# Batch 2's queries and keys by fp16 copies and transposed loads, and a new written order for the first part of a fused attention and MLP kernel

## The chip, the cores and the metric

The kernel runs on one core of a Trainium2 chip. The core has a matrix engine (TensorE, PE in the profile), VectorE (DVE), ScalarE (ACT), GpSimd (POOL) and SyncE (SP). DMAs are issued from queues of these engines; here POOL issues all loads that change fp32 into fp16, and SP the transposed loads and the stores. Sixteen DMA engines carry the data of all queues. The metric is the device time of one execution in microseconds.

## The reference

Eight batches, twelve heads, 448 positions and 64 numbers per head; then 3584 tokens of width 768 through an MLP with 2048 hidden units.

```python
scores = scale * np.matmul(q, k.transpose(0, 1, 3, 2))
m = np.max(scores, axis=-1, keepdims=True)
e = np.exp(scores - m)
attn = e / (np.sum(e, axis=-1, keepdims=True) + np.exp(-m) + 1e-09)
out = np.matmul(attn, v)
x = out.transpose(0, 2, 1, 3).reshape(B * S, H * D)
h = np.maximum(x @ w_in, 0.0)
return (h * h) @ w_out
```

The kernel takes the exponentials without the maximum, adds one to their sum (which is the same ratio), and takes the reciprocal as exp(-ln(...)).

## The kernel before, in words

All matmuls are in fp16, and everything is written out by hand: the schedule is manual, so each engine does its instructions in the order in which the program makes them. That order stands in two strings, `ORDER` (line 676) for the first part, called the front here, and `CYCLE` (line 750) for the rest. Each word of a string is a step, a letter with numbers, looked up in `STEPS` (line 637 for the front, line 732 in `period` for the cycle). `ORDER` holds attention of batches 0 to 3, the first layer of batches 0 and 1, and the output pieces 0 to 13. `CYCLE` is run twice, each time for attention of two more batches, the first layer of two earlier ones and 28 output pieces; what is then left is written as plain loops.

The steps that matter here:

- `T` (`transpose_one`, line 203) and `U` (`transposed_copy`, line 210): one quad is a group of four heads, so a batch has three. `T` transposes the queries or the keys of a quad on TensorE, 14 transposes into PSUM; `U` copies them out, on VectorE or ScalarE, into a batch's `qk` tile.
- `s` and `e`: scores of one chunk (64 keys of four heads) and their exponentials. `s0` to `s23` are batch 0's in halves. From 24 on there are seven per quad, so `s24` to `s44` are batch 1, `s45` to `s65` batch 2, `s66` to `s86` batch 3. Chunk c of a quad is its first step plus c. `quad_scores` (line 400) has two forms. A batch in `ON_PE` uses four matmuls of 448 columns a chunk. The others use eight of 224, as their planes hold even and odd positions apart; keys are read from planes 1 and 2, queries from plane 0, and the last chunk's keys from a separate tile `kms`.
- `a`, `S`, `Z`, `M`, `v`, `X`: the sums of exponentials (VectorE and TensorE), their logarithm and reciprocal (ScalarE), the product with the values (TensorE) and the normalised result (VectorE). Their number is that of the quad, with 0 to 2 for batch 1, 3 to 5 for batch 2 and 6 to 8 for batch 3. Batch 0 has its own letters, `p`, `b`, `y`, `z`, `n`, `x`.
- `j`, `k`, `l`: first layer, two of six products of a 128-wide block, then its relu and its square. `j0` to `j15` are batch 1, from `j16` on batch 0. `i`, `r`, `g` do the same for pairs of blocks of half of batch 0.
- `o`, `O`, `Q`: an output piece of 128 tokens and half the width, which takes 16 blocks (two per `o` step in the fine form), and its two-part eviction; `Q` stores from SP. There are four buffers for the evicted pieces.
- `d`: the loads of the list `LOADS` (line 626), by number.

Loads come in two forms. For batches in `ON_PE`, `load_quad` (line 618) brings a quad's queries and keys in natural layout to SBUF by POOL's queue. For the others, `stage` (line 144) copies the whole batch's queries and keys into fp16 tensors in DRAM by POOL's queue, and `transposed_load` (line 163) brings three planes of 0.69 MB (queries, keys, keys shifted by one position) from there by SP's queue. `tail_keys` (line 178) then makes `kms` from planes 1 and 2 by copies on POOL. A batch's `qk` tile has two buffers, so batch b's transposed loads wait for the last scores of batch b-2. The values have two buffers as well, and they take one or three DMAs for a batch in `ON_PE` and four for the others.

A step that issues on POOL or SP stands in that engine's queue of instructions. It is issued as soon as the steps before it on the same engine are done and what it needs is there, wherever it stands among the other engines' steps.

Of the kernel before, what the change touches and what calls it, by code (L numbers as in the profile page):

```python
# [16 lines left out]
def kernel(  # L17
# [160 lines left out]
    def tail_keys(b, planes=(1, 2)):  # L178

        if b not in kms:  # L180
            kms[b] = flat.tile([128, H, 64], FP16, name="flatq")
        km = kms[b]
        for which in planes:
            for r in range(2):
                rows_ = slice(64 * r, 64 * r + 64)
# [2 lines left out]
                nc.gpsimd.tensor_copy(km[rows_].rearrange("p h (x o) -> p h x o", o=2)[:, :, :, odd],  # L188
                                      src[:, :, S // 2 - 32:S // 2])
# [482 lines left out]
    def other_ring():  # L672
# [3 lines left out]
    ORDER = """
        d0 W8 d8 d1 c1,4,0 c0,0,1 t0,0,0 c1,0,1 t1,0,0 u0,0,0,0 t1,0,4 u1,0,0,0 c0,4,1 u1,0,4,1 t0,0,4 d2 s0 t0,1,0 u0,0,4,1 u0,1,0,0 t1,1,0 u1,1,0,0
        d10 d9 s1 t0,1,4 e0 t1,1,4 e1 s2 e2 u0,1,4,0 s12 e12 u1,1,4,0 T0,1,0 T0,1,1 U0,1,0,0,4,0 U0,1,1,0,4,0 U0,1,1,4,7,0 U0,1,0,4,7,0 s3 s4 p2 p0 e3
        b0,0 e4 s6 p1 d18 p3 s5 e6 e5 b0,1 b0,2 T0,2,0 b0,3 y0 T0,2,1 U0,2,0,0,4,0 z0 n0 U0,2,1,0,4,0 b1,0 s8 U0,2,0,4,7,0 U0,2,1,4,7,0 x0 d3 d17 d16
        b1,1 s9 d15 T1,0,1 e8 e9 U1,0,1,0,7,0 T1,0,0 U1,0,0,0,7,0 b2,0 s11 e11 s10 s13 e10 e13 s14 p8 b2,1 p4 d5 b2,2 p9 s7 e14 p10 b2,3 p11 y2 p5 e7  # L680
        z2 b1,2 p6 s15 b1,3 p7 e15 y1 b3,0 n2 x2 b3,1 z1 s17 e17 b3,2 p12 p13 b3,3 n1 s18 p14 s16 e18 p15 x1 y3 T1,1,0 U1,1,0,0,7,0 e16 b4,0 z3 b4,1
        s19 e19 i0,6 n3 r0,6,0 s20 e20 s21 i0,7 s22 x3 b4,2 e21 p16 b4,3 e22 b5,0 r0,7,0 p17 p18 p19 d4 b5,1 g0,6 y4 z4 n4 s23 T1,1,1 e23 d13 s27 b5,2
        x4 i0,4 s28 p20 p21 g0,7 b5,3 e27 p22 p23 y5 U1,1,1,0,7,0 e28 z5 r0,4,0 n5 x5 s26 s29 e26 j20,0,2 j23,0,2 j23,2,4 j20,2,4 j20,4,6 e29 j23,4,6
        s25 k23,1 s24 g0,4 e25 e24 k20,0 P0 i1,7 j19,0,2 l23 a0,0 s32 e32 a0,1 s36 d6 j19,2,4 e36 j16,0,2 l20 j19,4,6 j17,0,2 s34 s33 k19,1 r1,7,0
        j17,2,4 j16,2,4 a0,2 l19 e34 j17,4,6 e33 j16,4,6 g1,7 s30 d11 k16,1 s31 e30 k17,0 T2,0,0 T1,2,0 T2,0,1 T1,2,1 l16 s35 e31 U2,0,0,0,7,0
        U1,2,0,0,7,0 s37 U2,0,1,0,7,1 e35 j18,0,2 j18,2,4 e37 j18,4,6 a0,3 i1,6 d19 S0 U1,2,1,0,7,0 v0,0 a1,0 v0,1 Z0 v0,2 l17 v0,3 v0,4 v0,5 k18,0 d7
        d12 v0,6 s40 s43 M0 r1,6,0 j27,0,2 a1,1 e43 j22,0,2 j22,2,4 j27,2,4 X0 e40 j27,4,6 l18 j22,4,6 g1,6 a1,2 s39 k27,1 s38 e39 a1,3 d20 T2,2,0 e38
        k22,0 T2,2,1 T2,1,1 T2,1,0 s41 U2,2,1,0,7,1 U2,2,0,0,7,0 s42 j26,0,2 l27 e41 j21,0,2 j26,2,4 j26,4,6 l22 S1 U2,1,0,0,7,0 e42 U2,1,1,0,7,0 Z1
        v1,0 v1,1 v1,2 v1,3 v1,4 d23 v1,5 k26,1 v1,6 a2,0 a2,1 a2,2 s44 s47 M1 l26 e44 j21,2,4 d22 j21,4,6 i1,4 X1 a2,3 k21,1 v2,0 v2,1 v2,2 r1,4,0 S2
        e47 v2,3 Z2 v2,4 v2,5 l21 v2,6 M2 o0,0,4 s46 o0,4,8 d14 s50 e46 e50 o0,8,12 X2 o0,12,16 s51 g1,4 s48 O0,1 Q0 j15,0,2 j0,0,2 j15,2,4 j4,0,2  # L690
        j15,4,6 j4,2,4 j4,4,6 j0,2,4 e51 e48 j0,4,6 s45 k15,1 l15 o2,0,4 s49 e45 e49 o2,4,8 s52 d21 o2,8,12 a3,0 e52 o2,12,16 k4,1 k0,0 s53 a3,1 s55
        d24 j10,0,2 O2,1 j1,0,2 Q2 j10,2,4 j1,2,4 j10,4,6 l0 j14,0,2 l4 j1,4,6 j11,0,2 e55 k10,0 j14,2,4 a3,2 j11,2,4 k1,1 j8,0,2 l10 j14,4,6 j11,4,6
        k11,1 j9,0,2 a3,3 j8,2,4 j9,2,4 e53 l1 j8,4,6 j9,4,6 k14,0 s57 l14 e57 l11 S3 Z3 v3,0 d25 v3,1 v3,2 v3,3 k9,0 k8,0 v3,4 v3,5 v3,6 M3 o1,0,4
        s54 o1,4,8 X3 s56 o1,8,12 o1,12,16 e54 a4,0 O1,0 s63 e56 o5,0,4 s58 o5,4,8 Q1 e63 a4,1 a4,2 s65 e58 a4,3 o5,8,12 e65 s60 o5,12,16 e60 O5,1 s59
        v4,0 v4,1 Q5 v4,2 v4,3 l9 S4 v4,4 e59 Z4 M4 v4,5 v4,6 o4,0,4 o4,4,8 s61 o4,8,12 o4,12,16 e61 s64 O4,1 X4 s62 j2,0,2 l8 Q4 j2,2,4 j2,4,6 j7,0,2
        k2,1 j5,0,2 e62 j7,2,4 j7,4,6 k7,0 l7 d27 j12,0,2 j6,0,2 e64 a5,0 j12,2,4 j5,2,4 l2 j5,4,6 k5,1 j6,2,4 j6,4,6 j12,4,6 a5,1 j13,0,2 j13,2,4
        j13,4,6 l5 a5,2 j3,0,2 j3,2,4 j3,4,6 k12,0 a5,3 s69 l12 k6,1 o3,0,4 l6 k13,1 k3,1 l3 S5 l13 o3,4,8 o3,8,12 o3,12,16 O3,0 Q3 e69 s70 Z5 s71 d26
        M5 v5,0 v5,1 v5,2 v5,3 e70 e71 v5,4 v5,5 v5,6 o9,0,2 o9,2,4 X5 o9,4,6 o9,6,8 s66 o9,8,10 s68 o9,10,12 o9,12,14 o9,14,16 e66 O9,0 o6,0,2 e68
        s67 s72 o6,2,4 o6,4,6 o6,6,8 e67 o6,8,10 Q9 a6,0 a6,1 e72 a6,2 s73 o8,0,2 o6,10,12 o6,12,14 o8,2,4 o6,14,16 s75 e73 O6,0 o8,4,6 o8,6,8 e75 s78
        Q6 o8,8,10 o8,10,12 a6,3 e78 o8,12,14 s79 o8,14,16 s77 v6,0 v6,1 v6,2 v6,3 e79 e77 v6,4 S6 v6,5 v6,6 Z6 M6 s74 O8,0 Q8 o7,0,2 o7,2,4 e74 X6  # L700
        o7,4,6 s76 e76 a7,0 o7,6,8 o7,8,10 o7,10,12 o7,12,14 a7,1 o7,14,16 s82 d28 o10,0,2 O7,1 o10,2,4 o10,4,6 Q7 o10,6,8 s80 a7,2 e82 o10,8,10
        o10,10,12 o10,12,14 o10,14,16 e80 s85 s83 o11,0,2 o11,2,4 e85 o11,4,6 o11,6,8 d31 O10,1 Q10 e83 s81 a7,3 d29 o11,8,10 o11,10,12 o11,12,14 e81
        o11,14,16 O11,1 Q11 s84 o12,0,2 s86 o12,2,4 o12,4,6 e84 e86 o12,6,8 o12,8,10 a8,0 o12,10,12 o12,12,14 o12,14,16 S7 a8,1 O12,0 o13,0,4 o13,4,8
        d30 o13,8,12 Z7 Q12 a8,2 o13,12,16 v7,0 v7,1 v7,2 v7,3 O13,1 v7,4 a8,3 v7,5 v7,6 M7 S8 Q13 v8,0 v8,1 Z8 v8,2 v8,3 M8 v8,4 v8,5 X7 v8,6 X8
    """
# [120 lines left out]
```

## Time and profile before

| what | value |
|---|---|
| median of 3 runs | 392.39 us (392.0 to 394.6) |
| the profiled execution, its time | 393.06 us |
| its span in the profile | 391.3 us |
| granted TensorE clock | 1.0 throughout |
| HBM read, written | 45.69 MB, 17.93 MB |

Engine names are those of the profile; PEld is the loading of weights into TensorE. q0 is the DMA queue of POOL, q1 that of SP. The DMA share is the mean busy share of the sixteen DMA engines. It can exceed 1 as packets overlap. The sizes of loads are counted as they arrive, in fp16. In a timeline, a line is a run of like instructions with its start, its length, and in brackets the idle time before it and what ended that. A matmul's duration there reaches past the start of the next one, so the cost of one is taken from start to start.

### The profile page before, as it was taken

The numbers are of one execution on the slowest core, as the hardware profiler recorded it, in microseconds if no ns is written. First come the engines' busy times: TensorE is split into PE (matmuls) and PEld (weight loads), VectorE is DVE, ScalarE is ACT, GpSimd is POOL, SyncE is SP. The second block draws the span as 40 slices with busy tenths as digits, with TensorE's granted clock in tenths as the row PEclk, the third lists the DMA queues.
The fourth block names the chain that finished last, engine by engine and source line by source line (L and its number), as shares of the span: only waits on it lengthen the run. The fifth ranks groups of instructions, "written<-read, shape, count | busy, mean of one in ns | idle before, by whom it ended". The sixth has DMA issues, their size and how long they took to land.

```text
span 391.3 us, 14259 instructions
## 1 busy us (share of the span) xinstructions
PE 383.2 (98%) x6432; PEld 253.7 (65%) x6432; DVE 251.9 (64%) x468; ACT 228.5 (58%) x308; POOL 62.2 (16%) x96
## 2 busy tenths in 40 slices
PE   9789999999999999999999999999999999999997
PEld 5566656565789755667777665667777755556665
DVE  2887995765666766556968757566778788880000
ACT  5999998586689511349988731248988730001221
POOL 8544420025000701300001240310000000000000
PEclk9999999999999999999999999999999999999999
DMA  8999999999939899903129596941112200001132
GB/s 143 203 205 205 202 203 205 182 182 175 215 75 175 158 195 149 160 2 66 44 54 194 145 182 131 151 46 44 52 55 64 64 23 2 0 0 61 62 82 80
DMA packets 75052, 45.34 MB, mean 116 GB/s; under 512 B 47472, under 2 KB 72944, under 8 KB 74992
## 3 DMA queue, kind: packets, MB, share of 16 engines
q0 software_dynamic: 24752, 22.62, 37.4%
q1 hardware_dynamic: 49952, 21.59, 28.1%
q8 instruction: 50, 0.82, 0.9%
q10 hardware_dynamic: 288, 0.23, 0.2%
q14 instruction: 10, 0.08, 0.1%
HBM read 45.69 MB, written 17.93 MB: 163 GB/s over the span
## 4 chain that ended last, share of the span: by engine, by line
PE 86%; ACT 6%; DMA 2%; SPq 2%; DVE 1%; issue 1%; POOL 1%; ACTq 0%; POOLq 0%; DVEq 0%
PE mp L93 77%; PE sp L93 8%; ACT et L254 4%; SPq L166 2%; DMA nn<-in_k_dram 2%; PE mp L207 1%; DMA out_dram<-ot 1%; ACT rcp L372 1%; ACT nn L254 0%; DVE qk L217 0%; ACT rcp L365 0%; ACT ot L575 0%; DVE half L341 0%; ACT rcp L463 0%; DVE half L447 0%
## 5 line engine op out<-in xcount | busy, mean ns | idle before, releaser
L93 PE MATMUL mp<-wout,gs 64*64 64x384 f16 (+2 forms) x2928 | 165.2, 322 | 0.0
L93 PE MATMUL mp<-xt,win 128*64 128x448 f16 (+2 forms) x1188 | 148.3, 347 | 0.1
L93 PEld LDWEIGHTS <-gs 64*64 64x64 f16 (+1 forms) x2928 | 103.1, 106 | 34.5
L93 PEld LDWEIGHTS <-win 128*64 128x64 f16 (+1 forms) x1188 | 83.2, 106 | 63.5 <-issue 4.2
L254 ACT ACTIVATE et<-sp 128x896 f16<-128x896 f32 (+2 forms) x131 | 110.6, 889 | 12.3 <-PE sp L93 11.7
L505 DVE TENSOR_SCALAR rt<-mp 128x448 f16<-128x448 f32 x87 | 54.1, 622 | 17.4 <-PE mp L93 14.5
L509 DVE TENSOR_TENSOR gs<-rt 128x448 f16<-128x448 f16 x128 | 47.8, 390 | 22.1 <-ACT rt L503 20.2
L503 ACT ACTIVATE rt<-mp 128x448 f16<-128x448 f32 x41 | 21.8, 543 | 65.0 <-PE mp L93 55.7
L575 ACT ACTIVATE ot<-mp 128x384 f32<-128x384 f32 (+2 forms) x31 | 14.9, 480 | 71.6 <-PE mp L93 68.8
L93 PE MATMUL sp<-qk 64*64 64x224 f16 (+1 forms) x1056 | 53.7, 274 | 2.1 <-DVE qk L217 0.5
L93 PEld LDWEIGHTS <-qk 64*64 64x64 f16 x1056 | 32.7, 115 | 15.2 <-issue 6.5
L188 POOL COPY flatq<-qk 64x384 f16<-64x384 f16 x20 | 14.8, 739 | 172.7 <-DMA qk<-stage_k 126.0
L254 ACT ACTIVATE nn<-sp 128x896 f16<-128x896 f32 x42 | 37.1, 916 | 4.3 <-PE sp L93 4.2
L487 DVE TENSOR_TENSOR xt<-mp,rcp 128x448 f16<-128x448 f32 x42 | 24.2, 619 | 15.7 <-ACT rcp L466 10.3
L581 DVE SCALAR_TENSOR_TENSOR ot<-mp,ot 128x384 f32<-128x384 f32 x42 | 23.4, 556 | 15.3 <-ACT ot L575 12.4
L93 PEld LDWEIGHTS <-vn 64*64 64x64 f16 x756 | 22.4, 107 | 10.4 <-issue 1.8
L93 PE MATMUL mp<-et,vn 64*64 64x448 f16 (+1 forms) x448 | 24.5, 343 | 0.0
L577 DVE TENSOR_SCALAR ot<-mp 128x384 f32<-128x384 f32 x26 | 14.4, 555 | 14.3 <-PE mp L93 14.2
L463 ACT ACTIVATE rcp<-sp,one_b 128x896 f32<-128x896 f32 x21 | 21.1, 1007 | 2.8 <-PE sp L93 2.7
L466 ACT ACTIVATE rcp<-rcp 128x896 f32<-128x896 f32 x21 | 19.9, 949 | 0.5
L441 DVE TENSOR_TENSOR half<-et 128x1792 f16<-128x1792 f16 x15 | 16.3, 1088 | 4.3 <-ACT et L254 4.2
L443 DVE TENSOR_TENSOR half<-half,et 128x1792 f16<-128x1792 f16 x15 | 16.3, 1086 | 0.3
(59 smaller groups left out, 197.4 us busy)
## 6 DMA issues: line engine op xcount, KB each, us to landing
out_dram<-ot SPq DMA_DIRECT2D x52, 96.0 KB, 2.9
out_dram<-ot SPq DMA_DIRECT2D x19, 192.0 KB, 1.9
win<-in_moe_w_in_dram POOLq DMA_DIRECT2D x8, 384.0 KB, 12.3
wout<-in_moe_w_out_dram POOLq DMA_DIRECT2D x4, 768.0 KB, 14.9
vn<-in_v_dram POOLq DMA_DIRECT2D x10, 288.0 KB, 8.4
stage_q<-in_q_dram POOLq DMA_DIRECT2D x4, 676.0 KB, 13.1
stage_k<-in_k_dram POOLq DMA_DIRECT2D x4, 676.0 KB, 15.9
nn<-in_q_dram POOLq DMA_DIRECT2D x8, 224.0 KB, 8.6
```

The lines of the kernel that those rows point to most:

```text
L93: return nc.tensor.matmul(out_, lhsT, rhs, start=start, stop=stop)
L254: nc.scalar.activation(out=out_, in_=in_, func=AF.Exp, scale=scale)
L441: nc.vector.tensor_add(esq[m], a[:, 0:w], a[:, w:2 * w])
L443: nc.vector.tensor_add(esq[m], esq[m], z[:, 0:w])
L463: nc.scalar.activation(out=rcp, in_=zp[:, :, 0:S], func=AF.Ln, bias=one_b)
L466: nc.scalar.activation(out=zqs[m], in_=zqs[m], func=AF.Exp, scale=-1.0)
L487: nc.vector.tensor_mul(xts[b][:, 2 * g + i, :], xqs[m][i][:, 0:S], zqs[m][:, i, :])
L503: nc.scalar.activation(out=rt[:, 0:m], in_=hp[:, 0:m], func=AF.Relu)
L505: nc.vector.tensor_scalar(out=rt[:, 0:m], in0=hp[:, 0:m], scalar1=0.0, scalar2=None, op0=ALU.max)
L509: nc.vector.tensor_mul(gs[:, f0:f0 + per, t0 % RING:t0 % RING + n], r, r)
L575: nc.scalar.activation(out=ot, in_=op[:, 0:w], func=AF.Copy, scale=OUT_SCALE)
L581: nc.vector.scalar_tensor_tensor(out=ot, in0=lo[:, 0:w], scalar=OUT_SCALE, in1=ot, op0=ALU.mult, op1=ALU.add)
```

## The change

`ON_PE` loses batch 2: `load_quad`, `T` and `U` of batch 2 go, and `stage`, three transposed loads and the tail copies take their place. Batch 2's scores, values and stores take the second form. `LOADS` is made anew, with the transposed loads and the tail copies as steps of their own. `ORDER` is written anew.

```diff
-    ON_PE = (0, 1, 2)
+    ON_PE = (0, 1)
...
         x = {(0, 1): (0, 0), (0, 2): (0, 1), (1, 0): (1, 0), (1, 1): (0, 0), (1, 2): (0, 1),
-             (2, 0): (1, 0), (2, 1): (1, 1), (2, 2): (0, 0)}[b, g]
...
-    LOADS = ([lambda b=b, g=g: load_quad(b, g) for b in range(3) for g in range(NQ) if b + g]
+    LOADS = ([lambda b=b, g=g: load_quad(b, g) for b in range(2) for g in range(NQ) if b + g]
              + [lambda b=b, g=g: load_v_quads(b, g, g + 1) for b in range(2) for g in range(NQ)]
-             + [lambda: load_v_quads(2)]
              + [lambda i=i: load_win(i, NW) for i in range(NW)]
-             + [lambda n0=n0, y=y: load_wout(n0, y, 2) for n0 in (0, HALF) for y in range(2)]
-             + [lambda: stage(3), lambda: transposed_loads(3), lambda: tail_keys(3), lambda: load_v_quads(3),
-                lambda: stage(4), lambda: transposed_loads(4), lambda: tail_keys(4), lambda: load_v_quads(4), lambda: stage(5)])
+             + [lambda n0=n0, y=y: load_wout(n0, y, 2) for n0 in (0, HALF) for y in range(2)])
+    for b in (2, 3, 4):
+        LOADS += [lambda b=b: stage(b), lambda b=b: load_v_quads(b)]
+        LOADS += [lambda b=b, i=i: transposed_load(b, i) for i in range(3)]
+        LOADS += [lambda b=b, i=i: tail_keys(b, (i,)) for i in (1, 2)]
+    LOADS += [lambda: stage(5)]
```

The load numbers mean:

| load | before | after |
|---|---|---|
| quads of batches 0 and 1 (queries and keys) | d0 to d4 | d0 to d4 |
| quads of batch 2 | d5 to d7 | none |
| values of batches 0 and 1 by quads | d8 to d13 | d5 to d10 |
| `win` quarters | d15 to d18 | d11 to d14 |
| `wout` quarters | d19 to d22 | d15 to d18 |
| batch 2: stage, values, planes 0, 1, 2, tail copies of planes 1, 2 | values d14 | d19, d20, d21, d22, d23, d24, d25 |
| batch 3: the same | d23, d26, d24 (all planes), d25 (all tails) | d26, d27, d28, d29, d30, d31, d32 |
| batch 4: the same | d27, d30, d28, d29 | d33, d34, d35, d36, d37, d38, d39 |
| batch 5: stage | d31 | d40 |

Taken out of the two strings, the loads stand in these orders:

| queue | before | after |
|---|---|---|
| POOL | d0 d8 d1 d2 d10 d9 d18 d3 d17 d16 d15 d5 d4 d13 d6 d11 d19 d7 d12 d20 d23 d22 d14 d21 d25 d27 d26 d31 d29 d30 | d0 d5 d1 d2 d7 d6 d14 d3 d13 d12 d4 d11 d8 d9 d19 d10 d18 d15 d17 d24 d16 d20 d26 d25 d33 d40 d31 d32 d38 d39 d27 d34 |
| SP, with the stores around them | Q0 d24 Q2 ... Q9 Q6 Q8 d28 Q7 | d22 d21 d23 Q0 d30 Q1 Q2 d29 d28 Q5 Q6 Q3 d36 Q4 d37 Q7 d35 Q8 |

In the new string the rest of batch 0's first layer stands among attention 1. Batch 1's first layer then follows with no attention beside it. Attention of batches 2 and 3 comes after that, with the output pieces 0 to 13 among it. In the string of before, attention of batch 2 stands among batch 1's first layer and the first output pieces, and attention of batch 3 among the later ones. Three stretches of the new string:

```diff
+        M2 v2,4 X1 v2,5 v2,6 X2 j27,0,2 j27,2,4 j27,4,6 j11,0,2 j11,2,4 j15,0,2 j15,2,4 k27,1 j11,4,6 j2,0,2 j2,2,4 l27 k11,0 j5,0,2 j15,4,6 j0,0,2
...
+        j12,2,4 k4,0 j13,0,2 j12,4,6 l9 j13,2,4 j13,4,6 k7,1 s48 s45 o0,0,2 l4 o0,2,4 o0,4,6 o0,6,8 e48 s49 o0,8,10 d20 e45 o0,10,12 o0,12,14 l7 e49
...
+        o4,0,2 a5,1 s65 Z4 O3,1 e65 Q3 o4,2,4 o4,4,6 o4,6,8 o4,8,10 o4,10,12 o4,12,14 a5,2 o4,14,16 d36 O4,0 v4,0 v4,1 s69 Q4 s67 v4,2 v4,3 v4,4 M4
```

`CYCLE`, the loops behind it and the functions that make the steps are unchanged.

More of the change, by code (lines that the diff above doesn't have):

```diff
@@ L618, in load_quad @@
     def load_quad(b, g):
-        x = {(0, 1): (0, 0), (0, 2): (0, 1), (1, 0): (1, 0), (1, 1): (0, 0), (1, 2): (0, 1),
-             (2, 0): (1, 0), (2, 1): (1, 1), (2, 2): (0, 0)}[b, g]
+        x = {(0, 1): (0, 0), (0, 2): (0, 1), (1, 0): (1, 0), (1, 1): (0, 0), (1, 2): (0, 1)}[b, g]
         if (b, x[0]) not in nats:
@@ L676 @@
     ORDER = """
[L677 to L704, printed above, removed]
+        d0 c0,0,1 d5 d1 c1,4,0 W8 t0,0,0 d2 c1,0,1 t1,0,0 u0,0,0,0 t1,0,4 c0,4,1 u1,0,0,0 t0,0,4 u1,0,4,1 s0 t0,1,0 u0,0,4,0 e0 t1,1,0 u0,1,0,0 s1 e1
@@ new lines @@
+        u1,1,0,0 t0,1,4 t1,1,4 u0,1,4,0 s2 s12 u1,1,4,0 T0,1,0 T0,1,1 e2 U0,1,0,0,4,0 U0,1,1,0,4,0 e12 s3 U0,1,1,4,7,0 s4 p0 e3 e4 b0,0 p2 s5 s7 b0,1
+        b0,2 p3 p1 b0,3 y0 e5 e7 z0 s6 e6 U0,1,0,4,7,0 T0,2,1 U0,2,1,0,4,0 T0,2,0 s15 e15 U0,2,0,0,4,0 b1,0 n0 U0,2,1,4,7,0 U0,2,0,4,7,0 s8 e8 x0 s9
+        e9 T1,0,0 d7 s11 T1,0,1 s10 b1,1 p8 e11 e10 s14 e14 U1,0,0,0,7,0 s13 U1,0,1,0,7,0 b1,2 b2,0 d6 p4 p5 p6 b2,1 b1,3 e13 p7 y1 z1 p9 b2,2 p10 d14
+        d3 b2,3 p11 y2 b3,0 z2 n2 s19 b3,1 s16 e19 n1 x2 e16 s18 p12 b3,2 p13 x1 e18 p14 p15 s17 b3,3 e17 y3 i0,7 b4,0 z3 s21 s20 b4,1 i0,6 n3 e21 x3
@@ new lines @@
+        b4,2 r0,7,0 s22 b4,3 d13 p16 p17 e20 p18 b5,0 d12 e22 b5,1 s23 g0,7 b5,2 p19 y4 s27 z4 n4 i0,4 e23 x4 e27 s24 p20 b5,3 e24 p21 r0,6,0 d4 p22
+        p23 r0,4,0 y5 T1,1,1 z5 s28 g0,6 T1,1,0 U1,1,1,0,7,0 d11 n5 e28 s26 j20,0,2 x5 j20,2,4 d8 j20,4,6 U1,1,0,0,7,0 k20,0 e26 l20 s25 e25 g0,4 P0
+        d9 a0,0 s29 i1,6 e29 r1,6,0 s36 e36 d19 s32 T1,2,1 T1,2,0 s34 e32 d10 i1,7 j23,0,2 e34 U1,2,0,0,7,0 s30 e30 g1,6 r1,7,1 s33 e33 d22
+        U1,2,1,0,7,0 j22,0,2 j23,2,4 j23,4,6 j22,2,4 j16,0,2 k23,1 d21 s35 s31 g1,7 a0,1 j22,4,6 j16,2,4 e35 a0,2 e31 j16,4,6 s37 k22,0 v0,0 v0,1 a0,3
@@ new lines @@
+        e37 v0,2 l23 S0 v0,3 v0,4 v0,5 k16,0 s43 l22 j18,0,2 j21,0,2 a1,0 j18,2,4 Z0 v0,6 s40 e43 M0 s38 l16 j21,2,4 e40 X0 a1,1 j18,4,6 d18 j21,4,6
+        e38 j17,0,2 j17,2,4 k21,1 l21 k18,1 s39 s41 j17,4,6 e39 a1,2 a1,3 i1,4 e41 k17,1 s42 l18 a2,0 s44 e42 l17 r1,4,1 a2,1 j19,0,2 j26,0,2 j19,2,4
+        e44 j26,2,4 j19,4,6 d15 j26,4,6 a2,2 S1 k19,1 g1,4 d23 k26,0 a2,3 v1,0 v1,1 v1,2 v1,3 v1,4 Z1 M1 v1,5 v1,6 v2,0 v2,1 S2 v2,2 v2,3 Z2 l19 l26
+        M2 v2,4 X1 v2,5 v2,6 X2 j27,0,2 j27,2,4 j27,4,6 j11,0,2 j11,2,4 j15,0,2 j15,2,4 k27,1 j11,4,6 j2,0,2 j2,2,4 l27 k11,0 j5,0,2 j15,4,6 j0,0,2
@@ new lines @@
+        j2,4,6 d17 k15,0 l11 l15 k2,1 j5,2,4 j3,0,2 j0,2,4 l2 j5,4,6 j3,2,4 j3,4,6 j1,0,2 k5,0 l5 k3,1 j0,4,6 l3 j1,2,4 k0,1 j1,4,6 j8,0,2 d24 j8,2,4
+        j8,4,6 l0 j14,0,2 j14,2,4 j14,4,6 j9,0,2 j9,2,4 k8,0 k1,0 j7,0,2 l8 j9,4,6 k14,1 l1 l14 j4,0,2 j4,2,4 j12,0,2 j7,2,4 j4,4,6 k9,1 d16 j7,4,6
+        j12,2,4 k4,0 j13,0,2 j12,4,6 l9 j13,2,4 j13,4,6 k7,1 s48 s45 o0,0,2 l4 o0,2,4 o0,4,6 o0,6,8 e48 s49 o0,8,10 d20 e45 o0,10,12 o0,12,14 l7 e49
+        s46 k13,0 k12,0 o0,14,16 o1,0,2 o1,2,4 s50 e46 o1,4,6 s47 o1,6,8 o1,8,10 O0,0 e50 e47 d26 Q0 l13 o2,0,2 d25 s56 o1,10,12 s55 o1,12,14 o1,14,16
@@ new lines @@
+        e56 o2,2,4 o2,4,6 a3,0 d30 e55 O1,1 s54 s53 o2,6,8 a3,1 e54 o2,8,10 l12 Q1 o2,10,12 o2,12,14 o2,14,16 e53 a3,2 O2,1 s51 s52 Q2 e51 j6,0,2
+        j6,2,4 j10,0,2 j6,4,6 j10,2,4 a3,3 j10,4,6 S3 v3,0 k10,0 v3,1 v3,2 k6,1 e52 v3,3 v3,4 Z3 v3,5 M3 s57 o5,0,2 s60 o5,2,4 l6 o5,4,6 e57 e60 v3,6
+        o5,6,8 o5,8,10 o5,10,12 o5,12,14 s58 X3 a4,0 l10 o6,0,2 o5,14,16 o6,2,4 e58 s63 e63 O5,0 o6,4,6 a4,1 d29 s64 o6,6,8 o6,8,10 o6,10,12 d28
+        o6,12,14 o6,14,16 Q5 O6,0 d33 a4,2 s62 o3,0,2 e64 Q6 e62 s61 o3,2,4 e61 o3,4,6 o3,6,8 s59 e59 o3,8,10 a4,3 o3,10,12 o3,12,14 a5,0 S4 o3,14,16
@@ new lines @@
+        o4,0,2 a5,1 s65 Z4 O3,1 e65 Q3 o4,2,4 o4,4,6 o4,6,8 o4,8,10 o4,10,12 o4,12,14 a5,2 o4,14,16 d36 O4,0 v4,0 v4,1 s69 Q4 s67 v4,2 v4,3 v4,4 M4
+        v4,5 v4,6 e69 v5,0 v5,1 a5,3 S5 d40 v5,2 e67 v5,3 v5,4 v5,5 v5,6 Z5 X4 o7,0,2 M5 s68 s71 X5 d31 e71 o7,2,4 o7,4,6 o7,6,8 d37 o7,8,10 o7,10,12
+        o7,12,14 o7,14,16 e68 s70 e70 s75 o8,0,2 O7,0 o8,2,4 o8,4,6 e75 o8,6,8 o8,8,10 s66 d32 e66 o8,10,12 s72 o8,12,14 Q7 o9,0,2 o8,14,16 e72 s73
+        o9,2,4 o9,4,6 s76 o9,6,8 o9,8,10 e73 e76 d35 O8,0 o9,10,12 Q8 s74 o9,12,14 d38 s79 o9,14,16 a6,0 e74 o10,0,2 o10,2,4 o10,4,6 a6,1 O9,0 s78 Q9
@@ new lines @@
+        o10,6,8 o10,8,10 e79 s77 e78 a7,0 o10,10,12 o10,12,14 e77 s85 o10,14,16 o12,0,2 a7,1 e85 s83 o12,2,4 o12,4,6 s84 d39 O10,0 e83 o12,6,8
+        o12,8,10 s81 o12,10,12 o12,12,14 e84 a6,2 s80 e81 d27 e80 Q10 o12,14,16 a7,2 o11,0,2 a6,3 s82 o11,2,4 S6 o11,4,6 a7,3 O12,0 Q12 e82 a8,0
+        o11,6,8 o11,8,10 Z6 M6 o11,10,12 d34 o11,12,14 o11,14,16 O11,1 s86 v6,0 a8,1 v6,1 e86 v6,2 v6,3 v6,4 v6,5 v6,6 Q11 X6 a8,2 S7 v7,0 v7,1 v7,2
+        v7,3 v7,4 a8,3 v7,5 v7,6 o13,0,2 o13,2,4 o13,4,6 o13,6,8 o13,8,10 Z7 o13,10,12 M7 o13,12,14 X7 o13,14,16 v8,0 S8 v8,1 v8,2 O13,1 Q13 v8,3 Z8
@@ L705 @@
+        v8,4 M8 v8,5 v8,6 X8
     """
```

## The prediction

> **What bounds the kernel now.** I read the page first, then the chain of waits, busy time by stretches, the timelines of TensorE, GpSimd (POOL) and SyncE (SP), and the DMA view in short stretches.
>
> ```profile
> PE 383.2 (98%) x6432; PEld 253.7 (65%) x6432; DVE 251.9 (64%) x468; ACT 228.5 (58%) x308; POOL 62.2 (16%) x96
> DMA  8999999999939899903129596941112200001132
> GB/s 143 203 205 205 202 203 205 182 182 175 215 75 175 158 195 149 160 2 66 44 54 194 145 182 131 151 46 44 52 55 64 64 23 2 0 0 61 62 82 80
> PE 86%; ACT 6%; DMA 2%; SPq 2%; DVE 1%; issue 1%; POOL 1%; ACTq 0%; POOLq 0%; DVEq 0%
> ```
>
> TensorE (first line) is the bound over the span, and the chain (last line) is 86% TensorE. But the DMA lines (40 slices of 9.8 us) show a second resource that is full: until about 85 us the engines are busy throughout at some 200 GB/s. There, when data lands is a matter of its place in the queue.
>
> ```profile
> 20.00:30.00 10.00, 9.96 (x18) 1.00 1.24 204
> 30.00:40.00 10.00, 9.35 (x14) 1.00 1.26 205
> 40.00:50.00 10.00, 9.08 (x13) 1.00 1.27 197
> 50.00:60.00 10.00, 9.60 (x14) 1.00 1.19 209
> 42.80 1.75 PE L207 MATMUL mp<-ident,nn 128*64 128x128 f16 x56
> 44.48 0.57 PE L93 MATMUL sp<-qk 64*64 64x448 f16 x8
> 128.80 2.80 PE L93 MATMUL mp<-wout,gs 64*64 64x384 f16 x64
> 131.40 1.52 PE L93 MATMUL mp<-et,vn 64*64 64x448 f16 x28
> 135.02 0.73 PE L93 MATMUL sp<-qk 64*64 64x224 f16 x16
> ```
>
> The first four lines give ScalarE's busy time in each 10 us: from 10 to 60 us it has 47.7 of 50. The others are TensorE's timeline: 56 transposes from 42.80 to 44.48, an output piece of 64 matmuls from 128.80 to 131.40, and at 135.02 the first scores of `CYCLE`, where the front (`ORDER`) ends.
>
> **The front as a sum.** Along `ORDER` I add each step's matmuls at start-to-start durations from such rows: 0.19 us for a value or score chunk (0.25 for a chunk of batch 1 or 2 in before: eight matmuls take 0.50 in the chain in order of time), 0.38 for a `j` step of two products, 0.32 for an `o` step of two blocks, 0.42 for a `T` (1.68/4). Before: 122.9 us; the trace ends it at 135.0, so 12.1 us are start and waits. For ScalarE I add row durations (0.917 an exp, 1.007 and 0.949 the two steps of a normalisation, and so on): at `M2`, the end of attention 1, TensorE has 50.4 us of work behind it and ScalarE 62.3.
>
> **Removed.** Six `T` of batch 2, 84 transposes: 84 x 1.68/56 = 2.5 us of TensorE. Their copies out, four on VectorE (0.62 each) and two on ScalarE (0.93 each). The six `load_quad` DMAs of batch 2 are 1.38 MB in fp16.
>
> **Changed.** Batch 2's 21 score chunks become eight matmuls of 224 columns instead of four of 448. Sixteen such take 0.38 in the chain where eight of 448 take 0.50, so 21 x 0.06 = 1.3 us are gained (at worst 0). The new front sums to 119.1, 3.8 less.
>
> **ScalarE gives some back.** In the new order TensorE's work before `M2` is 45.9 and ScalarE's 59.6: it lags by 13.7 where it lagged by 11.9. As ScalarE is 95% busy there, TensorE should wait 1.8 us more (none to 2.5): 12.6 us lost at `M2` against 10.8. The 0.5 us of waits at 133 us (`M7` and `O13`, whose stores stood behind batch 4's transposed loads) and some 0.5 of slower steps around them should go, as those loads move elsewhere. Without any DMA trouble the front ends at 119.1 + 12.6 + 0.3 (what is left of the 1.3 lost after `M2`) = 132.0: -3.0 us.
>
> **Added.** On POOL: two stage copies (0.6 us of issue each), four issues for batch 2's values in place of one, four tail copies (0.74 each). POOL is 16% busy, so its time costs nothing; its order does. On SP and the DMA engines: three transposed loads, 2.06 MB. Stores of batch 2 need fewer DMAs, which is off the path.
>
> **Where the loads land.** This sets the end, I think. POOL issues in order and runs ahead of the text: before's stage 5 stands near the end of `ORDER` but was issued at 91.75, held only by tail copies that waited for planes.
>
> ```profile
> 82.02 1.29 POOL L188 COPY flatq<-qk 64x384 f16<-64x384 f16 x2 [30.35 <-DMA qk<-stage_k]
> ...
> 91.75 0.64 POOL L155 DMA_DIRECT2D stage_q<-in_q_dram  x1
> 135.72 15.96 SPq L166 DMA_TRANSPOSE qk<-stage_k  x1
> 151.78 3.82 SPq L166 DMA_TRANSPOSE qk<-stage_q  x1
> 155.65 3.50 SPq L166 DMA_TRANSPOSE qk<-stage_k  x1
> ```
>
> In the last three lines a plane of 0.69 MB holds SP for 16 us while a stage copy and a values load run, and 3.5 to 3.8 us after them. The DMA view says why: first 141 to 147 us, then 153 to 157.
>
> ```profile
> q0 software_dynamic: 321, 0.95, 94.8%
> q1 hardware_dynamic: 320, 0.08, 14.9%
> ...
> q1 hardware_dynamic: 4038, 1.03, 124.6%
> ```
>
> Packets, MB, share: q0 is POOL's, q1 is SP's. They go packet for packet, and a stage packet is 12 times as large: the plane gets 0.013 MB/us. Alone it gets 0.26. [...]
>
> New POOL queue: everything through batch 2's stage copy (new `d19`) is 8.19 MB. Before's queue landed its first 7.74 MB at 45.2 us by the trace's landings, at 0.202 MB/us, so `d19` lands at 47.4. Behind it come 0.23 of values and three `wout` quarters (2.36); tail copies of plane 1 (`d24`) wait; then `d16` (0.79), `d20` (0.69), stage 3 (`d26`, 1.38); tail copies of plane 2 (`d25`) wait; then at once `d33` and `d40`, stages 4 and 5 (2.75 in all), which nothing else holds. From 47.4 on, q0's 5.45 MB and batch 2's planes (2.06) at 0.195 MB/us end at 86: stage 3 has landed. Only then can SP start batch 3's planes (`d30`, stores `Q1` and `Q2`, `d29`, `d28`), against stages 4 and 5: 2.75 MB at 0.158 MB/us is 17.4 us, to 103.5. `d30` then has 0.46 MB left (1.8 us, SP free at 105), two stores take 1.2 us of SP each (107.4), two planes 3.6 each (114.6), and landing follows SP by about 2: **116 us**. Ends: 99, if planes lost nothing to q0, and 121, at the 88 GB/s of 147 to 153 us for the last part.
>
> `s69`, the first score of batch 3, reads all three planes and stands after 90.0 us of TensorE work; without a wait it starts at 102.6. It would wait 13.4 us, and every `o`, `v` and `s` behind it on TensorE with it, then VectorE and ScalarE. Forecast: -3.0 + 13.4 = +10.4 us on the front; what follows is unchanged. The profiled run is 393.06 (span 391.3), 0.2% over the median 392.39, and the difference goes on the median: **402.8**.
>
> If that wait is cut, `s48`, the first score of batch 2, is late next: 63.5 of work, due at 76.1. Its third plane (`d23`) shares with `wout` packets and `d16`; by bytes it lands between 75 and 82, so the wait is none to 6 us. It is inside the 13.4, as the loads do not wait for TensorE. Batch 3's values (`d27`, behind the tail copies of batch 4) would land near 138, when `v6,0` comes: none to 2 us.
>
> **Rivals.** *Planes keep up.* If the transposed loads ran at their lone 0.26 MB/us beside stage copies, batch 3's would land at 99 with the stores, before `s69`. Then -3.0: 389.4, and 387.6 if ScalarE gives nothing back. For it: 1.03 MB in 4 us at 153. Against it: the 16 us row. [...]
>
> *Shared by bytes.* If the queues halved 0.2 MB/us, 2.06 MB and 0.4 of stores need 24.6 us from 86 at most, less as q0 drains: 106 to 111, `s69` waits 3 to 8, 392.5 to 397.5. The `wout` mix (0.26 against 0.12 MB from 72 to 74 us) lies nearer to this.
>
> *Worse.* Both `s48` and the values wait, and stages 4 and 5 drain at 0.14: 121 and more, 407.8 or more.
>
> **Numbers.** 1% is 3.9 us, about what a measurement can tell. Forecast case 0.62 (396.5 to 407), shared by bytes 0.17 (most of it within 1%), planes keep up 0.16 (0.10 of it under 388.5), worse 0.05. Faster 0.10, same 0.20 (0.06 of planes keeping up and 0.14 of sharing), slower 0.70. The range, 389 to 407, leaves out the best outcomes and the worst case; the forecast's own is 396.5 to 407.
>
> **What would show it.** SP: the first transposed load of batch 3 holds the queue for over 10 us, near 87 to 105. DMA: q0 and q1 packet for packet there, q0 with over ten times the bytes. TensorE: a gap before a score matmul that reads `qk`, near 103 to 116, released by a DMA of `qk`; 140 `L207` matmuls instead of 224. Where that gap is under 3 us, the forecast is wrong, and with no gap at all planes kept up. A front that loses over 13 us by `M2` would show ScalarE's part larger than I have it.

## The result, and the profile after

The changed kernel takes 403.23 us (median of 6 runs, 401.65 to 409.54) against 392.6 us of the kernel before beside it: a ratio of 1.0252, 95% interval 1.0211 to 1.0293. The forecast was 402.8. The total came out within 0.5 us; its terms did not, as the experiments show. Medians here and below are of all runs, while ratios leave out slow ones (here the run of 409.54, whose granted clock was 0.983 where the other five had 0.990 to 0.992; their median is 402.2).

The profiled execution took 402.2 us, span 400.4. These lines of its page answer to the first ones shown of before (TensorE, the DMA engines in 40 slices, the chain's shares):

```profile
PE 384.2 (96%) x6432; PEld 257.3 (64%) x6432; DVE 252.2 (63%) x468; ACT 225.5 (56%) x302; POOL 62.0 (15%) x99
DMA  8999999999989999300226986970221210001222
GB/s 136 205 205 208 208 191 195 204 219 188 196 173 170 222 231 179 41 2 21 65 63 101 217 128 131 199 65 24 62 62 43 69 35 0 2 0 44 76 80 79
PE 88%; DMA 3%; DVE 2%; ACT 2%; SPq 2%; issue 1%; POOL 0%; POOLq 0%; DVEq 0%; ACTq 0%
```

The DMA engines are now full for 16 slices, up to 160 us, where before has a 3 in its twelfth (75 GB/s, now 173). TensorE's waits between 60 and 150 us (engine, line, releaser, us in all, times, longest):

```profile
PE sp L93 <- DMA qk<-stage_q: 5.4, 1, 5.4
PE sp L93 <- issue: 2.1, 2, 1.4
PE mp L93 <- issue: 0.3, 1, 0.3
```

The first is the forecast gap: `s69` waits for batch 3's planes. SP's timeline shows what held them:

```profile
85.48 15.15 SPq L166 DMA_TRANSPOSE qk<-stage_k  x1
100.73 2.83 SPq L549 DMA_DIRECT2D out_dram<-ot  x4
103.61 2.55 SPq L166 DMA_TRANSPOSE qk<-stage_k  x1
106.26 3.40 SPq L166 DMA_TRANSPOSE qk<-stage_q  x1
```

The first plane of batch 3 holds SP for 15 us, while stages 4 and 5 are copied (they land at 92.8 and 100.7), and the others take 2.6 and 3.4 us behind it. The DMA view from 88 to 98 us (queue, packets, MB, share) is the one the prediction was made from, at another place:

```profile
q0 software_dynamic: 620, 1.95, 97.6%
q1 hardware_dynamic: 538, 0.14, 10.2%
```

About packet for packet, and 14 times the bytes for POOL's queue. TensorE's timeline at the wait and at the end of the front (135.02 in before):

```profile
111.75 0.96 PE L93 MATMUL sp<-qk 64*64 64x224 f16 x16 [5.39 <-DMA qk<-stage_q]
...
143.13 0.66 PE L93 MATMUL sp<-qk 64*64 64x224 f16 x13
```

So 8.1 us of the 9.1 in the spans arise in the front. The other 1.0 is one gap put down to issue, at 144.5 us between the first scores of `CYCLE`; from there on TensorE stays 9.1 us behind to the end. Part of the 8.1 is the clock. These stretches give busy time of TensorE, weight loads, VectorE, ScalarE and POOL, then the granted clock, the DMA share and GB/s:

```profile
105.00:110.00 5.00, 1.15 (x19) 0.33 (x11) 2.65 (x5) 1.80 (x3) 0.68 (x2) 0.91 1.22 219
110.00:115.00 5.00, 3.25 (x44) 2.31 (x47) 0.32 (x1) 1.73 (x2) 1.75 (x3) 0.50 0.75 157
115.00:120.00 5.00, 5.00 (x124) 4.11 (x120) 2.14 (x5) 3.57 (x4) 0.00 (x0) 0.91 0.98 191
```

The clock is at a half from 109 to 116 us, some 4 us of it behind the wait: some 2 us more that the forecast didn't have.

### The profile page after: what moved, and what is told of

The parts are those of the page before. It is cut to its first block, busy times and chain, and to the rows that moved or that the text cites. A ratio compares the mean times of both kernels' runs of the same rounds, so it can differ in the third digit from the quotient of the medians.

```text
span 400.4 us, 14257 instructions
## 1 busy us (share of the span) xinstructions
PE 384.2 (96%) x6432; PEld 257.3 (64%) x6432; DVE 252.2 (63%) x468; ACT 225.5 (56%) x302; POOL 62.0 (15%) x99
## 4 chain that ended last, share of the span: by engine, by line
PE 88%; DMA 3%; DVE 2%; ACT 2%; SPq 2%; issue 1%; POOL 0%; POOLq 0%; DVEq 0%; ACTq 0%
PE mp L93 79%; PE sp L93 9%; DMA nn<-in_k_dram 2%; DMA qk<-stage_q 1%; ACT et L254 1%; SPq L166 1%; DVE qk L217 1%; PE mp L207 1%; SPq L549 1%; DVE half L343 0%; DVE half L341 0%; ACT rcp L372 0%; ACT rcp L365 0%; PE xp L93 0%; DVE half L347 0%
## 5 line engine op out<-in xcount | busy, mean ns | idle before, releaser
L93 PE MATMUL mp<-wout,gs 64*64 64x384 f16 (+2 forms) x2928 | 167.2, 322 | 0.3 <-issue 0.3
L93 PEld LDWEIGHTS <-gs 64*64 64x64 f16 (+1 forms) x2928 | 105.6, 106 | 31.7 <-issue 0.7
L93 PE MATMUL sp<-qk 64*64 64x224 f16 (+1 forms) x1116 | 54.9, 268 | 11.1 <-DMA qk<-stage_q 5.4
L509 DVE TENSOR_TENSOR gs<-rt 128x448 f16<-128x448 f16 x128 | 49.1, 400 | 22.5 <-ACT rt L503 20.6
L575 ACT ACTIVATE ot<-mp 128x384 f32<-128x384 f32 (+2 forms) x28 | 13.4, 478 | 72.0 <-PE mp L93 70.6
L93 PEld LDWEIGHTS <-qk 64*64 64x64 f16 x1116 | 36.8, 116 | 24.4 <-issue 16.6
L188 POOL COPY flatq<-qk 64x384 f16<-64x384 f16 x24 | 16.1, 673 | 184.4 <-DMA qk<-stage_k 183.7
L93 PEld LDWEIGHTS <-vn 64*64 64x64 f16 x756 | 23.8, 110 | 10.3 <-issue 1.1
L577 DVE TENSOR_SCALAR ot<-mp 128x384 f32<-128x384 f32 x29 | 16.1, 554 | 18.3 <-PE mp L93 18.1
L93 PE MATMUL mp<-et,vn 64*64 64x448 f16 (+1 forms) x448 | 26.0, 354 | 0.2 <-DVE ot L581 0.2
```

The costliest lines, as they stand in the source:

```text
L93: return nc.tensor.matmul(out_, lhsT, rhs, start=start, stop=stop)
L509: nc.vector.tensor_mul(gs[:, f0:f0 + per, t0 % RING:t0 % RING + n], r, r)
```

## The experiments

All compare with the kernel before on the same chip, whose median was 392.5 to 392.8 in these comparisons. "Front's end" is the start of the first score of `CYCLE` in the one profiled run.

| kernel | what it is | median us | ratio to before, 95% interval | front's end |
|---|---|---|---|---|
| changed kernel | | 403.23 | 1.0252 (1.0211 to 1.0293) | 143.13 |
| e1 | stages 4 and 5 late | 397.91 | 1.0121 (1.0097 to 1.0145) | 149.01 in a run of 407.1 |
| e2 | stage 5 late | 398.4 | 1.0131 (1.0108 to 1.0154) | 139.67 |
| e3 | e1, four relus on VectorE | 400.18 | 1.0143 (1.0104 to 1.0183) | 137.61 in a run of 395.7 |
| e4 | before, stages early | 395.76 | 1.0066 (1.0039 to 1.0094) | |
| e5 | e1, plane 2 of batch 2 protected | 404.78 | 1.03 (1.0273 to 1.0326) | 146.72 |
| e6 | e5, wide pieces | 400.34 | 1.0189 (1.0165 to 1.0213) | |
| e7 | before, wide pieces | 399.91 | 1.019 (1.016 to 1.0219) | |
| e8 | e5, eight buffers | 396.15 | 1.0089 (1.0068 to 1.0109) | 136.76 |
| e9 | new POOL order, eight buffers | 393.17 | 1.0024 (1.0011 to 1.0037) | 134.91 |
| e10 | before, eight buffers | 392.39 | 0.9992 (0.9981 to 1.0004) | |
| e11 | changed kernel, eight buffers | 401.79 | 1.0244 (1.021 to 1.0278) | 142.58 |
| e12 | POOL order of e9, four buffers | 403.21 | 1.0251 (1.0226 to 1.0275) | 145.79 |

**e1 and e2: is it the stage copies?** Only `ORDER` is edited, and in it the place of loads on POOL:

```diff
 POOL:
-d25 d33 d40 d31 d32 d38 d39 d27 d34    (changed kernel)
+d25 d31 d32 d33 d27 d38 d39 d34 d40    (e1)
+d25 d33 d31 d32 d38 d39 d27 d34 d40    (e2)
```

> The changed kernel with POOL's order alone changed: the tail copies of batch 3 (d31, d32) stand ahead of stage 4 (d33), batch 3's values (d27) follow it, and stage 5 (d40) comes last. TensorE's, ScalarE's and VectorE's orders and all bytes are the same. Theory (POOL runs ahead, and stages 4 and 5 starve batch 3's planes): the first plane of batch 3 holds SP some 3 us instead of 15.2, s69 does not wait, TensorE's clock does not dip, and the time is 389.5 (388 to 392). Rival (bytes: the DMA engines have too much to move in the front, so a wait only moves): the planes of batch 4 or the values come late instead, 398 or more. Rival (the written order of compute, attention of two batches in one stretch, is itself slow): TensorE waits for ScalarE in place of DMA, 398 or more.

> The changed kernel with stage 5 (d40) alone moved to the end of POOL's order; stage 4 stays ahead of the tail copies of batch 3. Theory (starving, packet for packet): one stage copy of 1.38 MB instead of two is in front, which is 7 to 8 us less; the first plane of batch 3 holds SP 7 to 9 us, the wait at s69 falls from 5.4 us to under 2, and the time is 392 (390 to 395). Rivals (bytes, or compute order): 399 or more.

The hold on SP is what was expected. In e2, with one stage copy beside it instead of two, SP's timeline and TensorE's waits have:

```profile
86.71 7.09 SPq L166 DMA_TRANSPOSE qk<-stage_k  x1
```

```profile
PE mp L93 <- issue: 2.6, 4, 1.7
PE mp L93 <- DMA vn<-in_v_dram: 1.3, 1, 1.3
PE sp L93 <- issue: 1.1, 2, 0.6
PE sp L93 <- DMA qk<-stage_q: 1.1, 1, 1.1
```

15.15 us with two stages, 7.09 with one, 4.55 in e1 and 2.40 in e3 with none; the wait of `s69` goes from 5.4 to 1.1 to none. The mechanism holds. The gain doesn't: 389.5 and 392 were expected, 397.9 and 398.4 came. The waits shown of e2 come to 6.1 us, and only 1.1 of them are for planes; 3.7 are gaps put down to issue (see the last section). In e1's profiled run another load had become late: `s48` waited 9.3 us for batch 2's third plane (`d23`), which shared the engines with `d16`, `d20` and `d26`. That is the slowest run of e1, so it doesn't explain the median.

**e4: the same in the kernel before.** Its stages 4 and 5 are put ahead of batch 3's tail copies.

```diff
 POOL:
-d21 d25 d27 d26 d31 d29 d30    (before)
+d21 d27 d31 d25 d26 d29 d30    (e4)
```

> The kernel before, with stages 4 and 5 (its d27 and d31) moved ahead of the tail copies of batch 3 (its d25) in POOL's order; nothing else is changed. Theory (starving): the planes of batch 3, issued at 67 us, share with 2.75 MB of stage copies and land near 100 instead of 86; the stores behind them on SP keep the buffers of evicted pieces, O4 waits near 92, and the time is 8 us more (5 to 12), 398 to 404. Rival (compute order): the same as before within 1 us. Rival (bytes): the same or less, as the same bytes are asked for earlier.

SP's first transposed load of batch 3, in before and then in e4:

```profile
67.23 9.40 SPq L166 DMA_TRANSPOSE qk<-stage_q  x1
```

```profile
67.36 22.60 SPq L166 DMA_TRANSPOSE qk<-stage_q  x1
```

The starving is there without anything else of the change. But `s69` then waited only 2.0 us, and the kernel lost 0.66%, some 2.6 us, where 5 to 12 were expected. The step from a plane's landing to the time is what I had too large.

**e3: ScalarE's share.** It ends four relus of attention 1 on VectorE (`k21,1`, `k17,1`, `k18,1` and `r1,4,1` become `,0`), on top of e1.

> The kernel of the first run, with four relus of batch 0's first layer beside attention 1 (blocks 17, 18, 21 and pair 4 of the second half) moved from ScalarE to VectorE, 0.54 us each off ScalarE and 0.62 each on VectorE. Theory (ScalarE's lag at the end of attention 1 is what the new order gives back): s48 is reached 1 to 2 us sooner than in the first run and the time is 0.8 to 2 us less. Rival (VectorE or the landing of batch 0's and 1's data sets the pace there): no change within 0.5 us, or up to 1.5 us more.

It isn't faster than e1 (400.18 against 397.91, intervals overlapping). From 50 to 60 us VectorE becomes the full engine (9.79 of 10 us, 9.15 in the changed kernel) and TensorE falls to 8.67. So this experiment doesn't measure ScalarE's lag; it only shows that VectorE has no room for it.

**e5 to e8: what costs the rest?** e5 takes `d23`'s rivals away. e6 and e7 change the form of the output pieces, e8 the number of evicted pieces.

```diff
 POOL:
-d17 d24 d16 d20 d26 d25 d31 d32 d33 d27 d38 d39 d34 d40    (e1)
+d17 d16 d24 d25 d20 d26 d31 d32 d33 d27 d38 d39 d34 d40    (e5, e6, e8)
 e6, e7, for the pieces of ORDER:
-                for y in (0, 64):
-                    for x, o in ((0, op), (64, lo)):
-                        mm(o[y:y + 64, 0:w], g[x:x + 64, y:y + 64], wout[x:x + 64, fb, n0:n0 + w],
+                mm((op, lo)[fb % 2][:, 0:w], g, wout[:, fb, n0:n0 + w], start=(fb < 2), stop=(fb >= NFFB - 2))
 e8:
-    osb_pool = ctx.enter_context(tc.tile_pool(name="osb", bufs=4))
+    osb_pool = ctx.enter_context(tc.tile_pool(name="osb", bufs=8))
```

> On top of the order of e1 (stages 4 and 5 late), POOL now also issues d16 before the tail copies of plane 1 (d24) and the tail copies of plane 2 (d25) before d20 and d26, so nothing new is on POOL's queue while batch 2's third plane (d23) loads. In every run d23 should hold SP under 5 us and land by 76, so the first score of batch 2 (s48) waits under 1 us, and the runs should lie within 2 us of each other. Theory A, the prediction's: DMA order is all that the change costs, so without both waits it gives -3.0: 389.5. Theory B: TensorE loses about 3 us in gaps in which it waits for its own instructions (each gap in the trace ends 2.3 to 2.7 us after a 16 KB packet of the instruction queue began), and about 2.5 us on evicted pieces near 130 to 140 us: 394 to 397.

> e5 with the 14 output pieces of the front as 16 matmuls of 128x128 weights and 384 columns each, even blocks into one accumulator and odd blocks into the other, in place of 64 matmuls of 64x64 weights: the same TensorE time by the rows (162.5 ns against 4 x 40.7), the same evictions and stores, but a quarter of the instructions for these pieces. Theory B: the gaps put down to issue go, 1 to 3.5 us less than e5. Rival: those gaps come from the DMA traffic or the score matmuls themselves and stay, within 0.7 us of e5. Second rival: wide matmuls between 64x64 ones cost TensorE something, slower than e5.

> The kernel before with the same wide output pieces in the front. Its trace shows no gap put down to issue, so theory B expects no change, 392.6 within 1 us. If wide pieces are faster by themselves, it is below 391.5 and e6 is no proof; if they cost something, it is above 393.6.

> e5 with eight buffers for evicted pieces instead of four. In the runs so far TensorE loses 2.4 to 2.7 us between 130 and 150 us, where the chain of waits goes through a store that landed 4 us after its issue and an eviction that waited for its buffer. If the buffers are the cause, 1 to 2.5 us less than e5 and a loss under 1 us there; if instructions or ScalarE are, within 0.7 us of e5.

e5 was the worst miss. Its third plane holds SP for 2.91 us, and `s48` doesn't wait, as expected; the runs lie within 2.6 us (2 expected). But the wait only moved. TensorE's waits from 40 to 150 us:

```profile
PE sp L93 <- DMA qk<-stage_q: 4.0, 1, 4.0
PE mp L93 <- ACT ot L575: 2.3, 1, 2.3
PE sp L93 <- issue: 1.7, 1, 1.7
PE mp L93 <- issue: 0.9, 2, 0.6
```

Behind `d25`, `d20` and `d26` land later, batch 3's first plane starts on SP at 92.4 instead of 85.5, and `s69` waits again. The second line isn't in the changed kernel: TensorE waits for the eviction of an output piece. e8 removes that wait by buffers, and 8.6 us with it: more than three times the 1 to 2.5 expected. Its `s69` also waits less, 1.5 us against 4.0, so the difference isn't the buffers' alone.

e7 refutes e6 as a measurement: wide pieces by themselves cost the kernel before 7.1 us. No gap put down to issue is left in e6, where e5 has 2.6 us of them, but what that is worth can't be read from it.

**e9 to e12: order and buffers, together and alone.** e9 puts the last quarter of `wout` and batch 2's values behind batch 2's tail copies, and stage 3 ahead of the values.

```diff
 POOL:
-d18 d15 d17 d24 d16 d20 d26 d25 d33 d40 d31 d32 d38 d39 d27 d34    (changed kernel, e11)
+d15 d17 d16 d24 d25 d18 d26 d20 d31 d32 d33 d27 d38 d39 d34 d40    (e9, e12)
 e9, e10, e11: osb_pool with bufs=8; e12: bufs=4
```

> Eight buffers for evicted pieces, and on POOL the order d15 d17 d16 d24 d25 d18 d26 d20 d31 d32 d33 d27 d38 d39 d34 d40: the last quarter of wout and batch 2's values go behind batch 2's tail copies, and stage 3 ahead of the values. By bytes at 0.2 MB per us d23 lands by 75, d18 by 79 (needed at 82), stage 3 by 87 (92 in e5), batch 2's values by 90 (needed at 95), batch 3's planes by 101. Neither s48 nor s69 should wait more than 0.5 us. e8 lost 1.5 us at s69 and about 0.6 of clock behind it, so about 2 us less than e8: 393 to 395, level with the kernel before or up to 0.6% above it. Rival: DMA bytes are short throughout, so another load (the values or d18) is late in its place and nothing is gained on e8's 396.2.

> The kernel before with eight buffers for evicted pieces. It loses 1.2 us between 130 and 140 us, at the two waits behind batch 4's planes. If buffers cause these, 0.7 to 1 us less: 391.6 to 392.1. If e8's gain was the buffers' everywhere, several us less.

> The changed kernel as it is, with eight buffers for evicted pieces. Its one wait on a buffer stands at 104.7 us, just ahead of the wait of 5.4 us for batch 3's planes, which takes up whatever is gained there. So 402.5 to 403.3, a gain of at most 0.7. Rival: buffers cost it as much as they cost e5 (8.6 us), then 395 to 398.

> The POOL order of e9 with the four buffers of the changed kernel, so the order on POOL is all that differs from the changed kernel. e9 lost 0.4 us between 130 and 150 us; e2 and e3, with four buffers and no plane late, lost 3.5 and 2.5 there. So 2 to 3 us over e9: 395 to 396.5. Rival: with no plane late, evictions are never held up by the stores and the buffers are worth nothing, as in the kernel before: 393 to 394. Second rival: they cost as much as between e8 and e5: 399 or more.

e9 fell in its range: 393.17, level with before but for 0.24%. It lost nothing at `s48` or `s69`; its waits from 40 to 150 us are a gap put down to issue and batch 2's values, needed at 90 us and 0.4 late:

```profile
PE sp L93 <- issue: 0.9, 1, 0.9
PE mp L93 <- DMA vn<-in_v_dram: 0.4, 1, 0.4
```

e10 shows that buffers are worth nothing measurable to the kernel before (0.15 us, where 0.5 to 1 was expected), and e11 that they are worth at most a little to the changed kernel (1.4 us under its 403.23, a ratio of 1.0244 against 1.0252, with overlapping intervals). e12 is the surprise, where not the expectation but its second rival came true (399 or more): the order of e9 with four buffers costs 403.2, as much as the changed kernel. The four corners, medians in us:

| | four buffers | eight buffers |
|---|---|---|
| POOL order of the change | 403.23 | 401.79 |
| POOL order of e9 | 403.21 (e12) | 393.17 (e9) |

Either edit alone gives nothing or 1.4 us; both give 10.0 (9.0 by the ratios). e12's profile shows why. ScalarE's waits from 70 to 150 us, then TensorE's, then SP's timeline:

```profile
ACT ot L575 <- DMA out_dram<-ot: 6.9, 1, 6.9
```

```profile
PE mp L93 <- ACT ot L575: 4.2, 1, 4.2
PE mp L93 <- DMA vn<-in_v_dram: 1.3, 1, 1.3
```

```profile
116.91 4.14 SPq L166 DMA_TRANSPOSE qk<-stage_k  x1
121.14 1.18 SPq L549 DMA_DIRECT2D out_dram<-ot  x2
122.37 3.98 SPq L166 DMA_TRANSPOSE qk<-stage_k  x1
126.45 1.18 SPq L549 DMA_DIRECT2D out_dram<-ot  x2
127.73 3.49 SPq L166 DMA_TRANSPOSE qk<-stage_q  x1
131.32 15.54 SPq L549 DMA_DIRECT2D out_dram<-ot  x12
```

There is no wait for a plane any more, and TensorE reaches the steps behind `s69` four to nine us sooner than in the changed kernel. Its eviction `O11` stands on ScalarE and needs the buffer of piece 8, four pieces earlier. That is stored by `Q8`, which stands on SP behind `d35`, batch 4's last plane. SP is free at 131.3, the store lands at 136.7, and ScalarE has waited 6.9 us. TensorE needs the PSUM that `O11` empties, waits 4.2 us, and its clock falls to 0.81 and 0.85 in the two stretches of 10 us from 130 on. In the changed kernel the same planes hold SP from 114.9 to 127.6, but TensorE is late from `s69` and needs the buffer only after the store. The wait for planes hid the wait for buffers. In e12 this wait, smaller waits of 2.7 us more than e9's, and half the clock for 5.7 us behind the wait (2.8 us lost) make up 9.7 of the 10.9 us by which its front ends later than e9's.

The new POOL order has a part in this wait. In e9 and e12 stage 4 stands behind batch 3's tail copies and lands at 116.8 us (92.8 in the changed kernel), and batch 4's first plane starts right behind it, at 116.9. In e2 stage 4 stays early. Its first plane of batch 4 starts 7.3 us sooner than e12's:

```profile
109.66 3.38 SPq L166 DMA_TRANSPOSE qk<-stage_k  x1
```

With four buffers and only 1.1 us of waiting at `s69`, e2 has no wait for a store there, while e1, e3 and e5, with four buffers and stage 4 late, have one of 2.1 to 3.1 us on ScalarE. So "both edits are needed" holds for these two orders. An order with stage 4 early and batch 3's planes in time wasn't run.

## Why the total was right and its terms were not

**T, -2.5 us: right.** The `L207` matmuls are 140 instead of 224, and their busy time is 5.4 us instead of 8.0.

**Score form, -1.3 us: wrong.** The price of 0.25 us a chunk came from batch 1's chunks, beside whose matmuls TensorE waits. By starts, the 168 matmuls of 448 columns took 10.1 us in before, and the 84 that remain, batch 1's, take 5.8 in the changed kernel. That leaves 4.3 us for batch 2's 21 chunks, 0.205 each, if batch 1's cost the same in both. Against 0.19 in the new form that is 0.3 us at most.

**ScalarE's lag, 1.8 us: right.** The reciprocal `M2` began 59.3 us into the span with 45.9 us of TensorE's work ahead of it, in before at 62.1 with 50.4: 1.7 us more lag.

**The 133-us waits, -1.0 us: gone, for the wrong reason.** I had them go because batch 4's loads "move elsewhere". The loads didn't move away from the stores; TensorE was late for them. In e12, where `s69` doesn't wait, a wait of this kind is back, four times as large. In e2, where batch 4's planes start sooner, it isn't.

**Without DMA trouble, -3.0 us: wrong by 3 to 4.** e9 is that case, with eight buffers besides: +0.6 us, its front ending at 134.91 against 135.02, where 132.0 was forecast. Of the 3 us, 1.0 is the score form. The front still has 1.3 us in a gap put down to issue (0.9) and a wait for values (0.4) that the forecast had at nothing; the rest, some 0.6 us, I can't assign.

**`s69`'s wait, +13.4 us: the right place and cause, too large.** Stage 3 landed at 85.4 (86 forecast), the first plane held SP from 85.5 to 100.6 (86 to 105), and the last plane landed at 111.7 (116). By the prediction's step, stages 4 and 5 drain by 103.5 and two stores and two planes need 9.6 us of SP more; they drained by 100.7 and these needed 9.0. At the other end `s69` was due at 102.6 and TensorE reached it only at 106.4, since gaps put down to issue (1.7 us) and slower steps had cost 3.8 us on the way. So `s69` started 9.1 us after its due time, 5.4 of them in the wait. Half the clock then adds about 2, so the front ends at 132.0 + 9.1 + 2 = 143.1, as measured, where the forecast put it at 145.4. With eight buffers the change of POOL order alone is worth 8.6 us (e11 to e9).

**`s48` next, none to 6 us: right here, wrong as the next thing late.** It didn't wait: `d23` landed at 73.5, 1.5 us ahead of the forecast 75 to 82. In e1's profiled run it did, for 9.3 us. But with both settled, in e12, what is late next is a store behind batch 4's planes, on which the prediction had nothing left.

**The rivals.** "Planes keep up" and "shared by bytes" are refuted by the 15.15 us and by 538 packets against 620. The values of batch 3 didn't come late.

So, by the medians, -3.0 and +13.4 became +0.6 and +10.0 (e9 to the changed kernel; by the ratios +0.9 and +9.0): two errors of some 4 us against each other. That the total came within 0.5 us is luck; that a wait for batch 3's planes behind stages 4 and 5 would make the kernel slower is not.

## What to carry to other kernels

A transposed load in packets of some 0.26 KB beside a copy in packets of 3.1 KB got almost nothing here (0.14 MB of 2.09 in 10 us, 538 packets against 620), so it mattered what a runahead queue issued during such a load: the same plane held SP for 15.15 us with two stage copies beside it and for 7.09 with one, at the same bytes in all. When a wait is taken away, follow the same buffers and queues on to the next: here either of two edits alone was worth nothing or 1.4 us, and both were worth 9 to 10. A total that is right says little about its terms; run the term that is meant to be free by itself, as e9 did.

## What the runs showed of the hardware

**Gaps of TensorE behind packets of the instruction queue.** Between 60 and 150 us, gaps put down to issue appear in the middle of a step in every version of the changed kernel with narrow pieces, and not in before. TensorE's timeline in e2 has three of its six here:

```profile
82.37 0.52 PE L93 MATMUL mp<-wout,gs 64*64 64x384 f16 x7 [0.16 <-issue]
...
88.84 0.73 PE L93 MATMUL mp<-xt,win 128*128 128x448 f16 x3 [0.24 <-issue]
...
96.41 0.68 PE L93 MATMUL mp<-wout,gs 64*64 64x384 f16 x11 [1.71 <-issue]
```

In TensorE's sequence (weight loads and matmuls, with the few waits of its sequencer) these are instructions 2241, 2497 and 2753, 256 apart. Packets of 16,384 bytes of the instruction queue began at 80.0, 86.5 and 94.0. In nine profiles of the changed kernel and its versions, every such gap over 0.4 us from start to start in that stretch has a place with the same remainder by 256 (193, three times 194), and ends 2.2 to 2.7 us after such a packet began (in the changed kernel 2.3 us, at 94.6 and at 100.8, with packets at 92.3 and 98.5). That TensorE waits there for its instructions is inferred from these two regularities. Call the 256 instructions from one such place to the next a block. Where matmuls were small, a block lasted 4.4 to 6.3 us. From 82 us on in before, the packet began at most 2.5 us into a block that lasted under 5.5 us, and no gap followed. Before's one gap put down to issue, 0.5 us at 22.1 us, ended a block into which its packet began 3.8 us; the expectation of e7, that before's trace shows none, overlooked it. In the changed kernel the packet began 3.8 to 3.9 us into the blocks from 82 to 101 us, while the stage copies ran. That the copies delay the packet wasn't tried by itself. The gaps idle TensorE for 2.4 us in the changed kernel, 3.7 in e2 and 0.9 in e9.

**The granted clock fell at one wait.** With 5.4 us of waiting in the changed kernel it was 0.50 from 110 to 115 us, and with 4.2 us in e12 it was 0.81 and 0.85 in the two stretches of 10 us from 130 on. In e4 a wait of 2.0 us ended at 102.5; the clock was 0.86 from 100 to 105 us and 0.80 from 105 to 110, and 48 matmuls of an output piece took 3.63 us from 103.54 on, where 64 take 2.60 in before at 128.80. With e2's wait of 1.1 us and e8's of 1.5 the run's mean stayed at 1.0. So the waits of 2.0, 4.2 and 5.4 us cost more than their length.

**Wide pieces among narrow matmuls were dear.** In e7 a wide matmul starts 163 ns after another, but a 64x64 score starts 256 ns after a wide one (29 times), and a wide one 188 ns after a score of 224 columns (13 times) and 306 ns after one of 448 (12 times). With its 14 pieces cut up so by the attention steps the kernel takes 7.1 us more, though 16 wide matmuls in a row (16 x 163 ns, 2.6 us) take no longer than 64 narrow ones (2.60 us in before at 128.80). That these changes of form are all of the 7.1 us wasn't worked out.
